# Keys and queries of a head pair loaded onto the two halves of the partitions, in a kernel of chunk-selected attention and soft mixture of experts

## The chip, the cores and the metric

The kernel runs on one core of a Trainium2 chip. The metric is the device time of one execution in microseconds (us). TensorE (PE) multiplies matrices, PEld is its loading of stationary operands, VectorE is DVE, ScalarE is ACT, GpSimd is POOL (which also issues all loads here), and SyncE (SP) issues the stores. Every engine works through its own list of instructions in order; between engines there are only semaphores.

## The reference

Attention first. For 4 batches, 8 heads, 768 rows and head size 64, the keys of a head are cut into 24 chunks of 32 rows. Each query takes an upper bound of its score against each chunk, keeps the 6 best causal chunks, and attends to the causal keys in them.

```python
k_min, k_max = k_chunks.min(axis=3), k_chunks.max(axis=3)
ub = sum(maximum(q * k_min, q * k_max), axis=-1)      # -1e9 where the chunk is in the future
top_chunks = argsort(ub)[..., -6:]
scores = scale * q @ k.T                              # -1e9 where not selected or not causal
out = softmax(scores) @ v
```

Then a soft mixture of experts over x, the 3072 x 512 result: logits = x @ phi for 32 slots, a softmax over rows makes slot inputs, 8 experts (512 to 1024 to 512, relu) work on 4 slots each, and a softmax over slots mixes their results into the 3072 x 512 output. The inputs are float32; the kernel works in bf16 on chip.

## The kernel before

The unit of work is a pair of heads, 16 pairs in all (`NPAIR`). The two heads share the 128 partitions: 64 head dimensions of each. For a pair the steps are:

- **LK, LQ, LV** (L150 to L163): POOL issues a load each for k, q and v, which casts float32 to bf16. k and q come in with partition p holding rows 6p to 6p+5 of each of the two heads, in a tile of their own (`k_in`, `q_in`, three buffers each).
- **KT and QT** (L212): twelve transposes each on PE, six row groups by two heads, into one PSUM tile (`tr_ps`, two buffers shared with other steps). **KE and QE** (L224): ACT copies that tile to `kT` or `qT` (64 dimensions of two heads by 768 rows), putting rows back into order; qT is negated.
- **KN and KX** (L234, L240): DVE reduces kT to the minimum and the maximum of each chunk. **BD** (L244) spreads these to the two heads, **QP** (L252) makes the positive part of q.
- **UB** (L260): PE makes the bounds out of qT, qp and bd. **SL, SH, UN** (L275 to L294): DVE finds the sixth largest with MAX8, POOL copies a column, DVE marks the chunks not selected. **NT, NC** (L296, L305): PE transposes the marks, DVE copies them to `nsT`.
- **S0 to S5** (L310): PE makes scores in six groups of 384 or 512 columns, with two matmuls of k and q (L317) and then two or more that add the mask out of `nsT` (L327), in a PSUM tile with two buffers. **E0 to E5** (L334): ACT takes the exponential. **A0 to A5** (L343): POOL clears the diagonal blocks.
- **P0 to P5** (L355): PE multiplies with v. **NO** (L374): DVE normalises into `x_sb`. **XT, XE**: PE transposes x, DVE copies it out; every fourth pair **LG, LC** add the logits.

The order is written out by hand. `PLAIN` and `ORDER` (L46 to L60) are lists of step names, one list for each iteration, and the code emits steps in that order, so each engine gets its own steps in it. Steps of different pairs stand in one iteration: in iteration i the scores are those of pair i, bounds and marks (UB to NC) those of pair i+1, transposes and chunk extremes (KT to BD) those of pair i+2, the k and q loads those of pair i+4, P those of pair i-1. The plain iterations 1 to 12 read

```python
PLAIN = """S0 KT S1 E0 A0 E1 LQ NO UB S2 S3 P0 KE LK SL P1 P2 P3 P4 E2 E3 A2 A1 W XT SH QT UN S4 S5 QE LV KN E4
E5 A5 A3 XE KX NT P5 NC BD QP A4 LG LC"""
```

so that ACT gets E0 E1 KE E2 E3 QE E4 E5, DVE gets NO SL UN KN XE KX NC BD QP, and PE gets S0 KT S1 UB S2 S3 P0 to P4 XT QT S4 S5 NT P5. Iterations -2, -1, 0 and 13 to 16 have lists of their own.

Expert weights (step W, L136) are loaded one matrix at a time among the iterations, 1 MB in bf16 each; 12 of the 16 have room from the start, the other four are loaded as attention buffers are given back. In w1 a partition gets two runs of two rows. After the last pair come the dispatch of the mixture (L474, which reads x with a stride of two elements as the stationary operand, to match w1), the experts (L721 to L789) and the output (L792 to L818).

## Time and profile before

| | before |
|---|---|
| times of two runs | 163.35 and 163.38 us, median 163.37 |
| span of the profiled execution, first to last instruction | 161.6 us |
| median less span | 1.77 us |
| busy: PE, DVE, ACT, POOL | 139.9, 110.3, 121.6, 95.1 us |
| mean granted TensorE clock | 0.954 |
| bytes by DMA (as landed) | 32.95 MB |

The span is what the profile shows of one execution; what is outside of it (1.77 us) is start and end of the program, and no time of that execution is listed apart from the two runs. In the rows of the timeline the first number is the start in us, the second the length in us, then engine, line, operation, out<-in with shapes, and xN for N instructions of the same kind merged; a bracket tells idle time before it and what ended it. A row without a bracket did not wait.

### The profile page before, as it was taken

What the parts mean: (1) busy time and instruction counts of PE and PEld (TensorE: products, weight loads), DVE (VectorE), ACT (ScalarE), POOL (GpSimd) and SP (SyncE); (2) the same over time, 40 slices, a digit from 0 to 9 for tenths busy, and PEclk for the clock granted to TensorE, in tenths of its full rate; (3) what the DMA queues carried; (4) which work ended last, traced back from release to release, by engine and by line L of the source; (5) the groups of instructions that cost most, each with busy time, mean ns of one, the idle gap of its engine ahead of it and who ended that gap; (6) DMA issues with size and microseconds to landing.
All of it is one profiled execution on the core that took longest, in us unless ns stands there. A gap on an engine that the chain in (4) does not pass through costs nothing.

```text
span 161.6 us, 6418 instructions
## 1 busy us (share of the span) xinstructions
PE 139.9 (87%) x2705; PEld 100.2 (62%) x2705; DVE 110.3 (68%) x379; ACT 121.6 (75%) x157; POOL 95.1 (59%) x193
## 2 busy tenths in 40 slices
PE   6559899999899999999999999999999699985500
PEld 3345566767677777666867767775689545853200
DVE  5456678879698798887888879899655432176520
ACT  3386899999899999999998999987992112085510
POOL 7968788968789687896777976685454500000000
PEclk9999999999999999999999999999999959999555
DMA  3999999999999999999999999999999998029996
GB/s 51 159 172 196 175 211 196 212 195 184 212 194 214 191 184 214 185 216 192 186 205 190 214 188 218 194 208 186 214 214 217 214 214 162 16 103 404 405 407 243
DMA packets 40477, 32.95 MB, mean 204 GB/s; under 512 B 26369, under 2 KB 34561, under 8 KB 40449
## 3 DMA queue, kind: packets, MB, share of 16 engines
q0 software_dynamic: 38432, 26.25, 109.5%
q1 hardware_dynamic: 2016, 6.29, 9.9%
q8 instruction: 21, 0.34, 0.8%
q14 instruction: 8, 0.06, 0.1%
HBM read 52.49 MB, written 6.29 MB: 364 GB/s over the span
## 4 chain that ended last, share of the span: by engine, by line
PE 54%; POOL 15%; ACT 10%; DMA 7%; issue 6%; DVE 2%; DVEq 0%; POOLq 0%; ACTq 0%
PE sc_ps L317 10%; PE at_ps L369 9%; PE sc_ps L327 7%; PE tr_ps L218 6%; POOL e_sb L345 6%; ACT e_sb L340 6%; DMA out_dram<-o_sb 5%; PE ub_ps L266 4%; PE h_ps L725 3%; DMA q_in<-in_q_dram 3%; POOL k_in L155 3%; POOL w_sb L148 2%; PE xT_ps L391 2%; POOL q_in L155 2%; PE ns_ps L299 2%
## 5 line engine op out<-in xcount | busy, mean ns | idle before, releaser
L340 ACT ACTIVATE e_sb<-sc_ps 128x768 bf16<-128x768 f32 (+1 forms) x96 | 83.2, 925 | 4.1 <-PE sc_ps L327 3.6
L345 POOL TENSOR_SCALAR_AFFINE_SELECT e_sb<-e_sb 128x256 bf16<-128x256 bf16 x96 | 36.7, 404 | 26.4 <-ACT e_sb L340 24.8
L317 PE MATMUL sc_ps<-qT,kT 64*128 64x384 bf16 (+3 forms) x288 | 39.8, 295 | 1.2 <-ACT e_sb L340 0.9
L327 PE MATMUL sc_ps<-nsT,smask 64*128 64x384 bf16 (+2 forms) x320 | 38.4, 279 | 0.2 <-issue 0.2
L369 PE MATMUL at_ps<-v_t,e_sb 128*128 128x65 bf16 x672 | 27.9, 194 | 0.3 <-issue 0.3
L369 PEld LDWEIGHTS <-e_sb 128*128 128x128 bf16 x672 | 23.9, 98 | 5.9 <-issue 5.2
L317 PEld LDWEIGHTS <-kT 64*128 64x128 bf16 x288 | 16.3, 94 | 8.5 <-issue 2.0
L327 PEld LDWEIGHTS <-smask 64*128 64x128 bf16 x320 | 17.1, 96 | 4.2 <-issue 1.2
L237 DVE TENSOR_REDUCE mm<-kT 128x24 bf16<-128x768 bf16 x16 | 15.1, 943 | 3.1 <-ACT kT L227 3.1
L160 POOL DMA_DIRECT2D v_t<-in_v_dram x16 | 16.5, 1034 | 0.0
L227 ACT ACTIVATE kT<-tr_ps 128x768 bf16<-128x768 bf16 x16 | 12.9, 806 | 4.0 <-PE tr_ps L218 4.0
L382 DVE TENSOR_TENSOR x_sb<-at_ps,inv 128x768 bf16<-128x768 f32 (+1 forms) x17 | 15.5, 910 | 0.6
L227 ACT ACTIVATE qT<-tr_ps 128x768 bf16<-128x768 bf16 x16 | 13.0, 815 | 2.8 <-PE tr_ps L218 2.6
L242 DVE TENSOR_REDUCE mm<-kT 128x24 bf16<-128x768 bf16 x16 | 15.1, 943 | 0.0
L282 DVE MAX8 mx_t<-ub_ps 128x8 f32<-128x16 f32 (+4 forms) x160 | 14.5, 164 | 0.0
L155 POOL DMA_DIRECT2D k_in<-in_k_dram x16 | 11.6, 726 | 1.4 <-POOLq L833 0.8
L155 POOL DMA_DIRECT2D q_in<-in_q_dram x16 | 11.5, 716 | 0.3 <-issue 0.2
L813 ACT ACTIVATE o_sb<-o_ps,cinv 128x512 f32<-128x512 f32 x12 | 7.9, 687 | 4.7 <-DMA out_dram<-o_sb 3.0
L278 DVE TENSOR_REDUCE mx_t<-ub_ps 128x2 f32<-128x8 f32 x16 | 2.7, 167 | 12.4 <-PE ub_ps L272 8.0
L218 PE MATMUL tr_ps<-ident,q_in 128*64 128x128 bf16 x192 | 9.1, 234 | 2.1 <-DMA q_in<-in_q_dram 1.2
L806 PE MATMUL o_ps<-so_sb,cT_all 128*128 128x256 bf16 x48 | 7.8, 288 | 3.5 <-DVE o_sb L811 2.9
L148 POOL DMA_DIRECT2D w_sb<-in_moe_w_dram x15 | 10.7, 716 | 0.1
(122 smaller groups left out, 217.0 us busy)
## 6 DMA issues: line engine op xcount, KB each, us to landing
w_sb<-in_moe_w_dram POOLq DMA_DIRECT2D x15, 1024.0 KB, 11.7
out_dram<-o_sb SPq DMA_DIRECT2D x10, 512.0 KB, 4.9
k_in<-in_k_dram POOLq DMA_DIRECT2D x16, 192.0 KB, 8.5
q_in<-in_q_dram POOLq DMA_DIRECT2D x16, 192.0 KB, 7.8
v_t<-in_v_dram POOLq DMA_DIRECT2D x16, 192.0 KB, 11.1
w_sb<-in_moe_w_dram POOLq DMA_DIRECT2D x2, 512.0 KB, 13.9
out_dram<-o_sb SPq DMA_DIRECT2D x4, 256.0 KB, 3.1
phi_sb<-in_moe_phi_dram POOLq DMA_DIRECT2D x1, 32.0 KB, 8.3
```

Source lines behind the costliest of these rows:

```text
L155: nc.gpsimd.dma_start(out=t, in_=src.rearrange("h (p g) d -> p h (g d)", p=P))
L160: nc.gpsimd.dma_start(out=v_t[i % NV][:, :, :, :D], in_=v[b, 2 * j:2 * j + 2].rearrange("h (g p) d -> p h g d", p=P),)
L218: nc.tensor.matmul(ps[h * 64:(h + 1) * 64, g, :], lhsT=src[:, h, g * D:(g + 1) * D], rhs=ident, is_transpose=True,)
L227: nc.scalar.activation(t.rearrange("d (p g) -> d p g", g=NQT), st.pop((nm + "ps", i)).rearrange("d g p -> d p g"), func=ACT.Copy, scale=-1 ...
L237: nc.vector.tensor_reduce(mm[:, 0, 0, :], kT, axis=AX.X, op=ALU.min, negate=True)
L242: nc.vector.tensor_reduce(st["mm", i][:, 1, 0, :], kT, axis=AX.X, op=ALU.max)
L317: nc.tensor.matmul(ps[:, h, c:c + w], lhsT=kT[r, kg * P:(kg + 1) * P], rhs=qT[r, qs], start=True, stop=False,)
L327: nc.tensor.matmul(ps[:, h, c + (f - t0) * P:c + (l - t0) * P], lhsT=smask[r, x, kg].rearrange("p a b -> p (a b)"), rhs=nsT[r, (f - x * NJ ...
L340: nc.scalar.activation(e[:, :, :w], st.pop(("scps", i, g))[:, :, :w], func=ACT.Exp, scale=-scale)
L345: nc.gpsimd.affine_select(out=e[:, :, :P], in_=e[:, :, :P], compare_op=ALU.is_ge, fill=0.0, base=0, pattern=[[0, 2], [1, P]], channel_mult ...
L369: nc.tensor.matmul(o, lhsT=st["e", i, g][:, h, c:c + P], rhs=v_t[i % NV][:, h, kg, :], start=(kg == 0), stop=(kg == t),)
L382: nc.vector.tensor_tensor(st["x", b][:, t0:t1, 2 * j:2 * j + 2, :].rearrange("p t h d -> p h t d"), at[:, :, :, :D], inv.broadcast_to([P, ...
```

## The change

From pair 2 on (`FIRST = 2`), k and q of a pair share one tile of twice the width: k on partitions 0 to 63, q on 64 to 127, and a partition holds twelve rows of each head rather than six. Each of the two loads of a pair then writes 64 partitions with runs twice as long. The twelve transposes called KT now take the row groups 0 to 5 of k and q together, those called QT the groups 6 to 11; the ACT copies after them write six of every twelve columns of kT and of qT, which are two halves of one tile. Pairs 0 and 1 are loaded and transposed as before, in halves of the same tiles. Both kT and qT now hold negated values, so the extremes swap their roles (max first, then the negated min), the mask's signs and the sign of the exponential's scale change, and the instruction kinds stay. The first expert matrix w1 is loaded with four rows, one run of 16 KB, for each partition; the dispatch reads x with a stride of four elements in place of two. The order lists are unchanged, and each engine gets the same number of instructions in the same order. The line numbers of the changed kernel lie 1 to 12 higher.

```diff
+    FIRST = 2
...
-            src = moe_w1[i].rearrange("(a p x) f -> p a (x f)", p=P, x=2)
-            dst = w_sb[i].rearrange("p (a f) -> p a f", a=NDG // 2)
+            src = moe_w1[i].rearrange("(p x) f -> p (x f)", x=NDG)
+            dst = w_sb[i]
...
-        t = inp.tile([P, 2, NQT * D], BF16, name=nm + "_in", tag=nm + "_in")
         src = {"k": k, "q": q}[nm][b, 2 * j:2 * j + 2]
-        nc.gpsimd.dma_start(out=t, in_=src.rearrange("h (p g) d -> p h (g d)", p=P))
-        st[nm, i] = t
+        if ("kq", i) not in st:
+            st["kq", i] = inp.tile([P, 2, 2 * NQT * D], BF16, name="kq_in", tag="kq_in")
+        if i < FIRST:
+            t = st[nm, i] = st["kq", i][:, int(nm == "q")].rearrange("p (h c) -> p h c", h=2)
+            nc.gpsimd.dma_start(out=t, in_=src.rearrange("h (p g) d -> p h (g d)", p=P))
+            return
+        half = slice(0, 64) if nm == "k" else slice(64, P)
+        nc.gpsimd.dma_start(out=st["kq", i][half], in_=src.rearrange("h (p g) d -> p h (g d)", p=64))
...
-        src = st.pop((nm, i))
+        if i < FIRST:
+            src, g0 = st.pop((nm, i)), 0
+        else:
+            src, g0 = st["kq", i], NQT * (nm == "q")
...
-                    ps[h * 64:(h + 1) * 64, g, :], lhsT=src[:, h, g * D:(g + 1) * D], rhs=ident,
+                    ps[h * 64:(h + 1) * 64, g, :], lhsT=src[:, h, (g0 + g) * D:(g0 + g + 1) * D], rhs=ident,
...
-        t = tp3.tile([P, S], BF16, name=nm + "T", tag=nm + "T")
-        nc.scalar.activation(
-            t.rearrange("d (p g) -> d p g", g=NQT),
-            st.pop((nm + "ps", i)).rearrange("d g p -> d p g"),
-            func=ACT.Copy, scale=-1.0 if nm == "q" else 1.0,
-        )
-        st[nm + "T", i] = t
+        if ("kqT", i) not in st:
+            kq = st["kqT", i] = tp3.tile([P, 2, S], BF16, name="kqT", tag="kqT")
+            st["kT", i], st["qT", i] = kq[:, 0], kq[:, 1]
+        kq, ps = st["kqT", i], st.pop((nm + "ps", i)).rearrange("d g p -> d p g")
+        if i < FIRST:
+            o = st[nm + "T", i].rearrange("d (p g) -> d p g", g=NQT)
+        else:
+            g0 = NQT * (nm == "q")
+            o = kq.rearrange("d y (p g) -> d (y p) g", g=2 * NQT)[:, :, g0:g0 + NQT]
+        nc.scalar.activation(o, ps, func=ACT.Copy, scale=-1.0)
...
-        nc.vector.tensor_reduce(mm[:, 0, 0, :], kT, axis=AX.X, op=ALU.min, negate=True)
+        nc.vector.tensor_reduce(mm[:, 0, 0, :], kT, axis=AX.X, op=ALU.max)
...
-        nc.scalar.activation(e[:, :, :w], st.pop(("scps", i, g))[:, :, :w], func=ACT.Exp, scale=-scale)
+        nc.scalar.activation(e[:, :, :w], st.pop(("scps", i, g))[:, :, :w], func=ACT.Exp, scale=scale)
...
-                xt = x.rearrange("p t h d -> p t (h d)").rearrange("p t (a c x) -> p t a x c", a=NDG // 2, x=2)
+                xt = x.rearrange("p t h d -> p t (h d)").rearrange("p t (c x) -> p t x c", x=NDG)
```

More of the change, by code (lines that the diff above doesn't have):

```diff
@@ L193 @@
             nc.gpsimd.affine_select(
-                out=squad, in_=squad, compare_op=ALU.not_equal, fill=-NEG, base=0,
+                out=squad, in_=squad, compare_op=ALU.not_equal, fill=NEG, base=0,
                 pattern=[[-CH, 2], [-64, 2], [-1, NCHUNK]], channel_multiplier=1,
@@ L197 @@
             nc.gpsimd.affine_select(
-                out=squad, in_=squad, compare_op=ALU.not_equal, fill=1.0, base=-NCHUNK,
+                out=squad, in_=squad, compare_op=ALU.not_equal, fill=-1.0, base=-NCHUNK,
                 pattern=[[-CH, 2], [-64, 2], [0, NCHUNK]], channel_multiplier=1,
@@ L241, in kmax @@
         kT = st["kT", i].rearrange("d (c x) -> d c x", x=CH)
-        nc.vector.tensor_reduce(st["mm", i][:, 1, 0, :], kT, axis=AX.X, op=ALU.max)
+        nc.vector.tensor_reduce(st["mm", i][:, 1, 0, :], kT, axis=AX.X, op=ALU.min, negate=True)
     def heads(i):
@@ L477, in dispatch @@
             for k, (x, t) in enumerate(tiles):
-                xt = x.rearrange("p t h d -> p t (h d)").rearrange("p t (a c x) -> p t a x c", a=NDG // 2, x=2)
+                xt = x.rearrange("p t h d -> p t (h d)").rearrange("p t (c x) -> p t x c", x=NDG)
                 nc.tensor.matmul(
-                    si[:, dg, :], lhsT=xt[:, t, dg // 2, dg % 2, :] if dg < NDG else ones_sq,
+                    si[:, dg, :], lhsT=xt[:, t, dg, :] if dg < NDG else ones_sq,
                     rhs=d_sb[:, k, :], start=(k == 0), stop=(k == n - 1),
```

## The prediction

> **What bounds the kernel now.** I read the page first: busy time, then the engines by slices.

> ```profile
> PE 139.9 (87%) x2705; PEld 100.2 (62%) x2705; DVE 110.3 (68%) x379; ACT 121.6 (75%) x157; POOL 95.1 (59%) x193
> ...
> ACT  3386899999899999999998999987992112085510
> ...
> PEclk9999999999999999999999999999999959999555
> ```

> Between slice 5 and slice 29 (20 to 120 us) ACT is busy eight to nine tenths or more; in the tail it hardly works. So the loop over pairs is ACT's, and the next view is ACT's timeline of one iteration, from QE (the copy of qT, L227) to the next one.

> ```profile
> 92.58 0.81 ACT L227 ACTIVATE qT<-tr_ps 128x768 bf16<-128x768 bf16 x1
> 93.29 3.21 ACT L340 ACTIVATE e_sb<-sc_ps 128x768 bf16<-128x768 f32 x4
> 96.39 0.81 ACT L227 ACTIVATE kT<-tr_ps 128x768 bf16<-128x768 bf16 x1
> 97.08 1.95 ACT L340 ACTIVATE e_sb<-sc_ps 128x1024 bf16<-128x1024 f32 x2
> 99.04 0.81 ACT L227 ACTIVATE qT<-tr_ps 128x768 bf16<-128x768 bf16 x1
> ```

> No row has a bracket: ACT never waits, and the period is its own work, 99.04 - 92.58 = 6.46 us: E4, E5, E0, E1 (93.29 to 96.39), KE, E2, E3, QE. One exponential of 1024 columns takes 0.98 of it (1.96 for two); the three of 768 take (3.10 - 0.98)/3 = 0.71 each; a copy takes 0.69 to 0.71 before the next starts.

> DVE in the same stretch:

> ```profile
> 91.19 0.94 DVE L237 TENSOR_REDUCE mm<-kT 128x24 bf16<-128x768 bf16 x1
> 92.12 0.56 DVE L402 COPY xT_sb<-xT_ps 128x768 bf16<-128x768 bf16 x1
> 92.59 0.94 DVE L242 TENSOR_REDUCE mm<-kT 128x24 bf16<-128x768 bf16 x1
> 93.80 0.36 DVE L307 COPY nsT<-ns_ps 128x384 bf16<-128x384 bf16 x1 [0.27 <-PE ns_ps L299]
> ...
> 94.24 0.36 DVE L257 TENSOR_SCALAR qp<-qT 128x768 bf16<-128x768 bf16 x1
> ```

> KN (L237) starts at 91.19, with KE long done and 1.39 us before QE even starts. That is the place to look at.

> **The change, part by part.**

> *The new wait.* Before, kT came whole out of KE. Now KE writes rows 0 to 5 of every twelve and QE the rest, so a chunk's extremes need both: KN must wait for QE to end, though the order lists are the same. In the iteration shown KN would move from 91.19 to 93.42, by 2.2 us. Behind it in DVE's queue stand XE, KX, NC, BD, QP and NO; NC's nsT is awaited by the mask matmuls of S0, these by E0 on ACT, BD and QP by UB on PE. That closes a ring: QE, KN, XE, KX, NC, S0, E0, ... QE. Its hops come from these rows:

> ```profile
> 11.14 0.81 ACT L227 ACTIVATE kT<-tr_ps 128x768 bf16<-128x768 bf16 x1 [0.45 <-PE tr_ps L218]
> ...
> 11.98 0.95 DVE L237 TENSOR_REDUCE mm<-kT 128x24 bf16<-128x768 bf16 x1 [0.15 <-ACT kT L227]
> ...
> 13.33 0.36 DVE L307 COPY nsT<-ns_ps 128x384 bf16<-128x384 bf16 x1 [0.39 <-PE ns_ps L299]
> ...
> 13.74 0.50 PE L327 MATMUL sc_ps<-nsT,smask 64*128 64x384 bf16 x2
> ```

> ```profile
> 94.30 0.34 PE L327 MATMUL sc_ps<-nsT,smask 64*128 64x384 bf16 x2
> 94.57 0.53 PE L218 MATMUL tr_ps<-ident,k_in 128*64 128x128 bf16 x12
> ...
> 95.33 0.23 PE L327 MATMUL sc_ps<-nsT,smask 64*128 64x128 bf16 x2
> ...
> 95.50 0.20 PE L266 MATMUL ub_ps<-bd,qT 128*128 128x48 bf16 x1
> ...
> 98.47 0.53 PE L218 MATMUL tr_ps<-ident,q_in 128*64 128x128 bf16 x12
> ```

> ```profile
> 104.15 0.94 DVE L237 TENSOR_REDUCE mm<-kT 128x24 bf16<-128x768 bf16 x1
> 105.01 0.94 DVE L242 TENSOR_REDUCE mm<-kT 128x24 bf16<-128x768 bf16 x1
> ...
> 106.98 0.34 DVE L307 COPY nsT<-ns_ps 128x384 bf16<-128x384 bf16 x1
> ...
> 108.28 1.51 ACT L340 ACTIVATE e_sb<-sc_ps 128x768 bf16<-128x768 f32 x2 [0.47 <-PE sc_ps L327]
> ...
> 113.95 0.36 DVE L307 COPY nsT<-ns_ps 128x384 bf16<-128x384 bf16 x1
> ```

> Count from the start of QE. KN starts 0.84 later (11.98 - 11.14, a copy and its hand-over). KN to XE 0.90 (0.93 in the row shown, with a gap), XE to KX 0.47 (92.59 - 92.12), KX to the next DVE step 0.86 (105.01 - 104.15 for the same reduction): NC starts at 3.07 and S0's mask matmuls 0.41 after it (13.74 - 13.33), at 3.48. Their results are there 0.34 later, and E0 starts at about 3.86 with the hand-over of 0.04 that QT to QE shows (98.47 + 0.53 to 99.04).

> From there two branches return to QE. On PE, S0's mask at 94.30 to QE at 99.04 is 4.74 (KT, S1, UB, S2, S3, P0 to P4, XT, QT): 3.48 + 4.74 = 8.22. On ACT, E1 waits for S1, which ends 95.33 + 0.23 - 94.30 = 1.26 after S0's mask starts, so E1 starts at 4.78; then E1 0.71, KE 0.69, E2 and E3 1.96: 8.14. UB needs QP, which starts 0.44 after NC (94.24 - 93.80) and ends 0.36 later, at 3.87; PE reaches UB at 3.48 + 1.20 = 4.68, so that is covered by 0.8 us. The period becomes 8.2 us, and ACT would idle 1.5 us of it before E0.

> QE starts at these times in iterations 0, 2 and 13:

> ```profile
> 18.97 0.81 ACT L227 ACTIVATE qT<-tr_ps 128x768 bf16<-128x768 bf16 x1
> ...
> 31.75 0.81 ACT L227 ACTIVATE qT<-tr_ps 128x768 bf16<-128x768 bf16 x1
> ...
> 105.35 0.84 ACT L227 ACTIVATE qT<-tr_ps 128x768 bf16<-128x768 bf16 x1
> ```

> Pair 2 is the first of the new kind, and its KN stands in iteration 0. From iteration 2 to 13 there are 11 periods: 11 x 8.2 = 90.2 instead of 73.6. From 1 to 2 no XE exists yet: 8.2 - 0.47 = 7.7. From 0 to 1 NC also stands ahead of KX: 7.7 - 0.86 = 6.9. These two make 14.6 instead of 12.78. Sum: (90.2 - 73.6) + (14.6 - 12.8) = 18.4 us.

> Behind iteration 13, KN (104.15, once more before QE) would start at QE + 0.84, that is 106.19 on the old scale: 2.0 us late. No DVE row from there to NC of the last pair (113.95) has a bracket, so the delay reaches that pair's scores: 2.0 us. The low end is iteration 14's E0: NC 3.68 after QE (0.84 + 104.15's own distance to 106.98, 2.83), E0 0.79 later, 4.46, instead of 108.28 - 105.35 = 2.93: 1.5 us. I take 2.0.

> *Copies with six of twelve columns written.* Reading is as before, writing is in 128 runs. The nearest rows with such writes:

> ```profile
> L340 ACT ACTIVATE e_sb<-sc_ps 128x1024 bf16<-128x1024 f32 x48 | 47.8, 1035 | 0.8 <-PE sc_ps L327 0.8
> L340 ACT ACTIVATE e_sb<-sc_ps 128x768 bf16<-128x768 f32 x48 | 38.6, 816 | 3.3 <-PE sc_ps L327 2.8
> ...
> L469 ACT ACTIVATE c_pad<-lg_all 128x288 bf16<-128x288 f32 x2 | 0.8, 444 | 0.0
> ```

> Contiguous writes cost (1035 - 816)/256 = 0.86 ns an element and 159 ns fixed, so 288 elements would take 405; written in 72 runs they took 444, 0.5 ns a run at most. 128 runs: between 0 and 70 ns a copy, twice in the ring. Taken as 0 (the same row also reads another memory); the high end is 2 x 0.07 x 13 = 1.8 us.

> *Loads.* KT needs k and q now.

> ```profile
> 5.55 0.72 POOL L155 DMA_DIRECT2D q_in<-in_q_dram  x1
> ...
> 14.81 0.85 PE L218 MATMUL tr_ps<-ident,k_in 128*64 128x128 bf16 x12
> ...
> 90.73 0.72 POOL L155 DMA_DIRECT2D k_in<-in_k_dram  x1
> ...
> DMA to landing us min/median/max: 3.4/8.5/11.0
> ...
> 55.00:80.00 25.00, 24.67 (x518) 17.96 (x513) 20.95 (x77) 24.52 (x31) 20.13 (x42) 1.00 1.48 195
> ```

> In the loop LQ is issued ahead of LK, so k stays the later one: issued at 90.73, used by the KT one period after 94.57, at 101.03, a lead of 10.3 us against a median landing of 8.5, and longer with a longer period: 0. For pair 2, q is issued at 5.55 and KT runs at 14.81: with the median it is there (14.05), with the maximum 1.7 late. Taken 0, high end 1.7. Without that cover each late load would add its lateness to one period. Half as many runs for a load are worth nothing while no engine of the loop waits for one; w1 in single runs neither, as it is used only after the last pair.

> *Stride four in the dispatch.* h_sb, read with stride four by L737, and x_sb, read with stride two:

> ```profile
> L479 PEld LDWEIGHTS <-x_sb 128*128 128x128 bf16 x96 | 3.0, 97 | 0.4 <-issue 0.3
> ...
> L737 PEld LDWEIGHTS <-h_sb 128*128 128x128 bf16 x8 | 0.5, 118 | 0.6 <-ACT h_sb L732 0.6
> ```

> At most 21 ns for each of 96 loads, 2.0 us if none overlapped; L737 lies where the clock is lower, so I take 0. Signs and extremes swap at equal instruction counts: 0.

> **Sum.** 18.4 + 2.0 = 20.4 us. The profiled span 161.6 becomes 182.0; with the 1.8 us by which the runs' median (163.4) exceeds the span: 183.8.

> **The rivals.**

> *The load stream becomes the bound (slower still).* The row 55 to 80 shows DMA engines busy all the time, 195 GB/s. A pair takes 195 GB/s x 6.7 us (73.6/11) = 1.31 MB with k and q at 0.39; if half the partitions meant half the rate, these would need 4.0 us in place of 2.0, and a pair 8.7: 11 x 0.5 = 5.5 us over the forecast, 189. Against it: weights are few in late iterations, and the rate may be set by reading, which the halves do not touch. [...]

> *The granted clock falls.* With 1.5 us idle in each period PE could lose its clock: the mask matmuls took 0.50 at 13.74 and 0.34 at 94.30, a factor 1.47. PE's 4.74 would become 7.0, the period 10.6, the time up to 183.8 + 11 x 2.4 = 210. Against it: the clock row stays 9 through the loop, and PE still works 6 us of 8.2.

> *The wait is hidden (no change).* If KN's lateness fitted into idle time of DVE and nsT still came before S0 needed it, the time stays near 163.4. Only 0.27 us of idle stands in the DVE rows before NC, against 2.2, so it decides only if KN does not in fact wait for QE.

> *The loads were the bound (faster).* If the stream set the pace and runs twice as long made k and q twice as fast, a pair would save half of their 2.0 us: 11 x 1.0 off 163.4, 152. It decides only where engines wait for loads, and ACT's rows in the loop show no wait at all.

> **How the numbers follow.** Forecast 0.79; load stream 0.07; clock 0.06; hidden 0.05; faster 0.03. The forecast's own range: period 8.05 to 8.3 (-1.7 to +1.1), end -0.5, copies +1.8, pair 2 +1.7: 181 to 188. I widen it to 178 and 191, which takes in the load stream and leaves out the clock, hidden and faster cases, 0.14 together. About 2% is what a measurement here tells from no change: faster 0.03, same 0.05, slower 0.92.

> **What would show it.** In the profile after: KN starts 0.03 us after QE ends, with a bracket that names ACT; ACT idles about 1.5 us before E0 in each iteration, waiting for the mask matmuls; QE to QE is 8.2 us in iterations 2 to 13; copies stay at 0.81 us; PE waits for no load; the tail from the last pair on keeps its length. It would be wrong if KN starts before QE ends, if QE to QE stays near 6.5, or if the copies or the PE steps grow.

## The result and the profile after

The changed kernel takes 192.1 us (median of two runs, 190.74 and 193.51) against 163.4 before: a ratio of 1.174, 95% interval 1.166 to 1.182. The forecast of 183.8 had the direction and most of the size; the range, 178 to 191, ends just below the result. The profiled execution took 190.74 us with a span of 189.0, the forecast span was 182.0, so 7.0 us are unaccounted for. Ratios here and below leave out runs more than 1.5% above the fastest of their kernel, medians do not, and five profiles (the swapped lists, the 64-column transposes, the tiny matmuls, and the early order with a late first weight, twice) are of such runs, so totals are not compared by their spans.

The page of the changed kernel: busy time, ACT and the clock by slices.

```profile
PE 148.3 (78%) x2704; PEld 105.0 (56%) x2705; DVE 111.8 (59%) x379; ACT 123.5 (65%) x157; POOL 92.3 (49%) x193
...
ACT  2558797886759696787769696767599212218530
...
PEclk9999999999699999999799997899699996999755
```

ACT, which stood at 8 and 9 through the loop, now falls to 5 to 7 in most slices, with the same work as before (123.5 us against 121.6): it waits. PE is busy 8.4 us longer with one matmul record fewer, and its clock row has dips in the loop, which the row of before had not. First the waits, on DVE's timeline of one iteration:

```profile
103.67 0.95 DVE L249 TENSOR_REDUCE mm<-kqT 128x24 bf16<-128x768 bf16 x1 [2.14 <-ACT kqT L244]
104.54 0.55 DVE L414 COPY xT_sb<-xT_ps 128x768 bf16<-128x768 bf16 x1
105.00 0.94 DVE L254 TENSOR_REDUCE mm<-kqT 128x24 bf16<-128x768 bf16 x1
105.86 0.34 DVE L319 COPY nsT<-ns_ps 128x384 bf16<-128x384 bf16 x1
```

and on ACT's, from one QE to the next:

```profile
102.82 0.82 ACT L244 ACTIVATE kqT<-tr_ps 128x768 bf16<-128x768 bf16 x1
103.53 1.72 ACT L352 ACTIVATE e_sb<-sc_ps 128x768 bf16<-128x768 f32 x2
106.72 1.71 ACT L352 ACTIVATE e_sb<-sc_ps 128x768 bf16<-128x768 f32 x2 [1.47 <-PE sc_ps L339]
108.32 0.81 ACT L244 ACTIVATE kqT<-tr_ps 128x768 bf16<-128x768 bf16 x1
109.02 1.94 ACT L352 ACTIVATE e_sb<-sc_ps 128x1024 bf16<-128x1024 f32 x2
110.98 0.82 ACT L244 ACTIVATE kqT<-tr_ps 128x768 bf16<-128x768 bf16 x1
```

QE (L244) ends at 103.64 and KN (L249) starts 0.03 us later, after 2.14 us of idle time that the bracket puts down to the copy. NC (L319) starts 3.04 us after QE, where the prediction counted 3.07, and E0 is 1.47 us late for the mask matmuls. QE to QE is 110.98 - 102.82 = 8.16 us, forecast 8.2. The ring is there, hop by hop, and the chain of work that ended last passes through these steps and back to QE by E0, E1, KE, E2 and E3.

From iteration 2 to 13 the eleven periods are 8.16, 9.68, 8.26, 8.17, 8.16, 8.17, 9.56, 8.17, 8.16, 9.65 and 8.01. Three of them are 1.4 to 1.5 us too long. The stretches view, for one ordinary period and those three (length, busy time and count of PE, PEld, DVE, ACT and POOL, then the granted clock, the DMA share and GB/s):

```profile
34.49:42.65 8.16, 6.57 (x136) 4.83 (x134) 5.75 (x20) 6.58 (x8) 4.67 (x11) 1.00 1.42 144
42.65:52.33 9.68, 8.09 (x136) 5.78 (x134) 5.69 (x20) 6.68 (x8) 6.60 (x14) 0.82 1.18 171
85.09:94.65 9.56, 8.04 (x136) 5.57 (x134) 5.72 (x20) 6.81 (x9) 5.24 (x11) 0.82 1.23 129
110.98:120.63 9.65, 8.05 (x136) 5.65 (x134) 5.70 (x20) 6.68 (x8) 5.63 (x12) 0.82 1.23 180
```

The same 136 matmuls take PE 6.57 us at clock 1.00 and 8.04 to 8.09 at 0.82, while DVE and ACT are busy about as long as in the first row. The clock changes in steps: in each of the three long periods it is 0.50 for one stretch of 3.41 us and 1.00 around it, and all its changes lie on a grid of 3.41 us. Four stretches of that grid:

```profile
44.50:47.91 3.41, 1.87 (x47) 1.40 (x46) 3.25 (x7) 1.85 (x3) 1.52 (x4) 1.00 0.85 166
47.91:51.32 3.41, 3.41 (x46) 2.35 (x45) 1.44 (x12) 2.98 (x4) 2.46 (x5) 0.50 1.50 185
...
68.39:71.80 3.41, 2.23 (x41) 1.50 (x36) 2.19 (x3) 2.79 (x4) 2.52 (x6) 1.00 0.90 133
71.80:75.22 3.42, 3.02 (x65) 2.10 (x65) 3.08 (x18) 2.47 (x4) 2.18 (x5) 1.00 1.02 204
```

The first holds PE's whole wait of 1.54 us for the mask (44.55 to 46.10): PE works 1.87 us, 0.55 of it, and the next stretch runs at half the clock. In the third the same wait (70.66 to 72.20) is cut by the border at 71.80: PE works 2.23 us, 0.65, and the clock stays. In the long period from 85.09 the idle time comes in two parts, 0.80 us that the profile gives to "issue" and 0.72 for the mask. The timeline shows where in the period, and, in its first three rows, what became of the iteration 0 to 1, which took 7.82 us in place of 6.9:

```profile
6.01 0.60 POOL L149 DMA_DIRECT2D w_sb<-in_moe_w_dram  x1
...
13.77 0.60 POOL L162 DMA_DIRECT2D kq_in<-in_q_dram  x1
...
22.54 0.53 PE L227 MATMUL tr_ps<-ident,kq_in 128*64 128x128 bf16 x12 [1.15 <-DMA kq_in<-in_q_dram]
...
49.70 1.80 PE L381 MATMUL at_ps<-v_t,e_sb 128*128 128x65 bf16 x30
...
109.02 1.12 PE L381 MATMUL at_ps<-v_t,e_sb 128*128 128x65 bf16 x30
```

The thirty P matmuls take 1.80 us in a dip and 1.12 outside of one. And KT of pair 3 at 22.54 waits 1.15 us for a load of q issued 8.8 us before, behind a whole expert matrix issued at 6.01; before, KT used k alone.

The 7.0 us: three dips 4.3 (9.68 + 9.56 + 9.65 - 3 x 8.2), iteration 0 to 1 0.9, the way from QE of iteration 13 (128.64) to the end 2.1 (60.4 instead of 56.25 + 2.0), the other periods -0.3. What stands behind each had to be tried.

### The profile page after: what moved, and what is told of

It is laid out like the page before. It is cut to its first block, busy times and chain, and to the rows that moved or that the text cites. A ratio compares the mean times of both kernels' runs of the same rounds, so it can differ in the third digit from the quotient of the medians.

```text
span 189.0 us, 6405 instructions
## 1 busy us (share of the span) xinstructions
PE 148.3 (78%) x2704; PEld 105.0 (56%) x2705; DVE 111.8 (59%) x379; ACT 123.5 (65%) x157; POOL 92.3 (49%) x193
## 3 DMA queue, kind: packets, MB, share of 16 engines
q0 software_dynamic: 33824, 26.25, 95.3%
## 4 chain that ended last, share of the span: by engine, by line
PE 30%; ACT 25%; DVE 19%; DMA 8%; issue 8%; POOL 5%; ACTq 0%; DVEq 0%; POOLq 0%
ACT e_sb L352 15%; ACT kqT L244 9%; DVE mm L249 7%; DVE mm L254 6%; PE sc_ps L339 5%; PE at_ps L381 5%; DMA kq_in<-in_q_dram 5%; PE sc_ps L329 4%; DMA out_dram<-o_sb 4%; DVE xT_sb L414 3%; PE h_ps L737 2%; PE tr_ps L227 2%; PE ub_ps L278 2%; DVE nsT L319 2%; PE at_ps L491 1%
## 5 line engine op out<-in xcount | busy, mean ns | idle before, releaser
L329 PE MATMUL sc_ps<-kqT 64*128 64x384 bf16 (+3 forms) x288 | 42.2, 311 | 1.0 <-ACT e_sb L352 0.9
L249 DVE TENSOR_REDUCE mm<-kqT 128x24 bf16<-128x768 bf16 x16 | 15.2, 953 | 34.9 <-ACT kqT L244 34.9
L244 ACT ACTIVATE kqT<-tr_ps 128x768 bf16<-128x768 bf16 x32 | 26.2, 819 | 9.5 <-PE tr_ps L227 9.3
L227 PE MATMUL tr_ps<-ident,kq_in 128*64 128x128 bf16 x384 | 18.8, 240 | 3.1 <-DMA kq_in<-in_q_dram 2.2
L329 PEld LDWEIGHTS <-kqT 64*128 64x128 bf16 x288 | 16.3, 97 | 8.5 <-issue 2.4
L227 PEld LDWEIGHTS <-kq_in 128*64 128x64 bf16 x384 | 13.2, 119 | 8.3 <-issue 5.0
L254 DVE TENSOR_REDUCE mm<-kqT 128x24 bf16<-128x768 bf16 x16 | 15.1, 943 | 0.0
L278 PE MATMUL ub_ps<-bd,kqT 128*128 128x48 bf16 x96 | 10.2, 192 | 1.2 <-DVE schunk L543 1.2
L278 PE MATMUL ub_ps<-bd,qp 128*128 128x48 bf16 x192 | 10.4, 190 | 0.4 <-ACT qp L267 0.4
L278 PEld LDWEIGHTS <-kqT 128*128 128x128 bf16 x96 | 8.3, 101 | 3.5 <-ACT kqT L244 1.4
L823 DVE TENSOR_SCALAR o_sb<-o_ps,cinv 128x512 f32<-128x512 f32 x11 | 8.0, 747 | 3.6 <-DMA out_dram<-o_sb 2.6
```

The costliest lines, as they stand in the source:

```text
L227: nc.tensor.matmul(ps[h * 64:(h + 1) * 64, g, :], lhsT=src[:, h, (g0 + g) * D:(g0 + g + 1) * D], rhs=ident, is_transpose=True,)
L244: nc.scalar.activation(o, ps, func=ACT.Copy, scale=-1.0)
L249: nc.vector.tensor_reduce(mm[:, 0, 0, :], kT, axis=AX.X, op=ALU.max)
L254: nc.vector.tensor_reduce(st["mm", i][:, 1, 0, :], kT, axis=AX.X, op=ALU.min, negate=True)
L278: nc.tensor.matmul(o, lhsT=w[:, t * P:(t + 1) * P], rhs=bd[:, x], start=(t == 0 and z == 0), stop=False,)
L329: nc.tensor.matmul(ps[:, h, c:c + w], lhsT=kT[r, kg * P:(kg + 1) * P], rhs=qT[r, qs], start=True, stop=False,)
```

## The experiments

Theory: the wait of KN for QE makes the period 8.16, and the 7.0 us are lost clock, in gaps that this wait makes, and one late load. Rivals: the half-partition loads or the interleaved copies cost something by themselves; the form of the first weights does.

**The wait without the change.** In the kernel before, KT and QT, and KE and QE, change places in the lists of iterations 0 to 13. Loads, copies and weights stay as they were; k's copy is now the later one, so KN must wait for it.

```diff
-PLAIN = """S0 KT S1 E0 A0 E1 LQ NO UB S2 S3 P0 KE LK SL ... SH QT UN S4 S5 QE LV KN E4
+PLAIN = """S0 QT S1 E0 A0 E1 LQ NO UB S2 S3 P0 QE LK SL ... SH KT UN S4 S5 KE LV KN E4
```

> The kernel before, with the names KT and QT, KE and QE exchanged in the lists of iterations 0 to 13: q is transposed and copied first, k second. Loads, layouts and copies are those of before; only KN now has to wait for the later copy. Ring theory: the same ring, a period of 8.2 us, and 184 to 190 us, the upper end if the TensorE clock also falls in some periods. Rival, the loss comes from loads or copies: 163 to 165 us.

Measured: 187.0, 195.9, 196.3 and 197.9 us, median 196.1, against 164.3 for the kernel before on that chip (no interval is given for it). Both kernels were run again beside each other on another chip:

> The kernel before, unchanged, profiled on the chip of this batch: on another chip its time spread from 163.2 to 169.3 us. All theories: ratio 1.00 within 1.5%, a period of 6.5 us, KN 1.4 us ahead of QE. If the KT of pair 3 waits for its k load here too, the wait of 1.2 us in the run with the new w1 belongs to the chip and not to w1; if not, to w1.

> The changed kernel, unchanged, on the chip of this batch, as the base for the other two: 189 to 194 us. Clock theory: the period is 8.2 us where the granted clock is 1.00 and 9.5 to 9.7 where it is near 0.82, and the number of the long ones differs from the first profile's three.

Measured: 164.5 us for the kernel before (ratio to its other runs 1.002, 0.995 to 1.009) and 194.8 us for the changed one, ratio 1.181, 1.170 to 1.192. The stretch from QE of iteration 1 to that of iteration 11, first the swapped, then the changed kernel:

```profile
28.31:116.61 88.30, 74.42 (x1390) 53.61 (x1388) 57.20 (x201) 66.15 (x81) 53.20 (x108) 0.90 1.13 152
```

```profile
28.61:116.92 88.31, 74.24 (x1390) 53.64 (x1388) 57.15 (x201) 66.22 (x81) 50.77 (x108) 0.90 1.10 151
```

Ten iterations take 88.30 and 88.31 us, at the same clock, with a first period of 7.69 and then periods of 8.15 to 8.17 and of 9.5 to 9.7 mixed in the same order. The wait alone, with the clock lost in its gaps, gives all of the loss in the loop; half-partition loads and interleaved copies add nothing to it. The swap was expected at 184 to 190. One run of four lies there, with a mean granted clock of 0.912; the three others are 6 to 8 us above, at 0.860 to 0.885, and the one of them that was profiled has six long periods of eleven, as the changed kernel beside it has, against the three of the first profile of the changed one.

**Part of the wait taken away.** The changed kernel with XE ahead of KN and KX behind NC on DVE.

```diff
-... S4 S5 QE LV KN E4 E5 A5 A3 XE KX NT P5 NC BD QP A4 LG LC"""
+... S4 S5 XE QE LV KN E4 E5 A5 A3 NT P5 NC KX BD QP A4 LG LC"""
```

> The changed kernel with two moves in the plain order list: XE goes ahead of QE's wait, KX behind NC, so that DVE gets UN XE KN NC KX BD QP. All of the change's loads, copies and waits stay. Ring theory: nsT is ready 1.7 + 0.36 us after QE starts instead of 3.1 + 0.36, E4 and E5 cover that, and the period falls from 8.2 to 6.5 or 6.6 us; with what lies outside the plain iterations (pair 3's wait for its loads 0.9, end of the loop 2 to 3, dispatch 0.8) the time is 166 to 169 us. Rival, the loads of half the partitions or the copies with gaps cost the time: it stays above 185.

Measured: 180.6 us, ratio 1.102 (1.094 to 1.109); the period is 7.43, not 6.5. DVE and one row of PE:

```profile
74.06 0.95 DVE L249 TENSOR_REDUCE mm<-kqT 128x24 bf16<-128x768 bf16 x1 [0.75 <-ACT kqT L244]
74.93 0.35 DVE L319 COPY nsT<-ns_ps 128x384 bf16<-128x384 bf16 x1
...
76.51 0.56 DVE L269 TENSOR_SCALAR qp<-kqT 128x768 bf16<-128x768 bf16 x1
...
77.12 0.22 PE L278 MATMUL ub_ps<-bd,qp 128*128 128x48 bf16 x2 [0.28 <-DVE qp L269]
```

NC (74.93) now comes right behind KN, ahead of KX, but QP has moved further back, and UB waits for it: 3.9 us from QE (73.21) to UB, 3.5 from there to the next QE. My expectation followed one branch of the ring, the one through NC, and missed the one through QP and UB, which the prediction had covered by 0.8 us.

**The clock.** The changed kernel with 24 matmuls more in S0 ahead of the mask, into columns of the PSUM tile that no step reads.

```diff
+    FILL = {i: 12 if i == 1 else 24 for i in range(1, 14) if i not in (6, 10)}
...
+            if g == 0:
+                for _ in range(FILL.get(i, 0)):
+                    nc.tensor.matmul(ps[:, 0, 384:512], lhsT=ident, rhs=ident, start=False, stop=False)
```

> The changed kernel with 24 matmuls of 128 columns (12 in iteration 1) into unused columns of S0's tile, between S0's products and its mask, in iterations 1 to 13 without 6 and 10: PE works through the 1.5 us in which it would wait for nsT. If the three periods of 9.6 us come from the granted clock, which falls after these waits, all 11 periods are 8.2 us and the time is 186 to 188 us. If they have another cause, they stay, and the time is 191 or more.

Measured: 189.1 us, ratio 1.151 (1.139 to 1.163). Ten of eleven periods are 8.01 to 8.27, and one is 9.31, with E0 2.21 us late in place of 1.47 and a stall of PE of 0.76 us that the profile gives to "issue"; from QE of iteration 2 to that of 13 it took 90.9 us, against 94.2 and 98.3 in the two profiles without fillers. But iteration 0 to 1 took 12.8 us, with KT of pair 3 waiting 4.0 for its q load at a low clock (0.74 on average from 18 to 26 us), which took part of the gain back and put the total above what the clock theory had said.

**The late load.** In the changed kernel, the first expert matrix is issued after q of pair 3 and not after q of pair 2.

```diff
-    -1: """UB KT KE SL UN QT SH NT LK QE KN PHI NC KX LQ QP BD""",
+    -1: """UB KT KE SL UN QT SH NT LK QE KN PHI NC KX LQ W0 QP BD""",
...
-    for n in "K0 Q0 K1 I Q1 K2 Q2 W G M V0 V1".split():
+    for n in "K0 Q0 K1 I Q1 K2 Q2 G M V0 V1".split():
```

> The changed kernel with the first weight matrix issued after pair 3's q load rather than after pair 2's: 2 MB less to read ahead of the loads that the KT of pair 3 waits for. If that wait (1.2 to 4 us in iteration 1) is part of the loss, it goes away and the time falls by 1 to 4 us against the changed kernel; if something else follows close behind, by less than 1.

Measured: 190.9 us, ratio 1.162 (1.152 to 1.172), 3.9 us below the changed kernel beside it. Its timeline:

```profile
13.36 0.60 POOL L162 DMA_DIRECT2D kq_in<-in_q_dram  x1
13.95 0.58 POOL L149 DMA_DIRECT2D w_sb<-in_moe_w_dram  x1
...
21.08 0.53 PE L227 MATMUL tr_ps<-ident,kq_in 128*64 128x128 bf16 x12
```

KT of pair 3 at 21.08 has no bracket, and iteration 0 to 1 takes 6.83 us; the forecast was 6.9. The swapped kernel, with whole loads and the old form of w1, also needs q first at this place, and there q's transposes wait 2.23 us for their load: the need for the later of the two loads is enough.

**Both repairs.** Fillers and late first matrix together.

> The changed kernel with both repairs that worked alone: the 24 filler matmuls in the gap ahead of S0's mask (iterations 1 to 13 without 6 and 10, 12 in iteration 1), and the first weight issued after the q load of pair 3. Theory (the forecast's mechanism was right and its sum left out the lost clock and the late load of pair 3, which are independent): iteration 0 to 1 near 7, periods of 8.15 to 8.3 in at least 10 of 11, and 184 to 187 us, near the 183.8 of the prediction. Rival (the two gains are one and the same, since the late load of pair 3 starts the row of clock losses, or the load only moves to a later pair): 188.5 or more, no better than the better of the two alone.

Measured: 184.2 us, ratio 1.129 (1.117 to 1.141). The forecast's 183.8 over 163.4 is 1.125. The stretch from QE of iteration 2 to that of iteration 11:

```profile
33.92:107.46 73.54, 70.79 (x1424) 54.59 (x1422) 51.85 (x182) 59.18 (x72) 45.34 (x97) 1.00 1.30 171
```

Nine periods in 73.54 us, 8.17 each, at clock 1.00; the two after them take 8.76, with a stall of PE of 0.50 us by "issue", and 8.01; iteration 0 to 1 takes 7.09, and from QE of iteration 13 to the end 58.2 us, where the forecast was 56.25 + 2.0. The gains add up, so they are two things, and with both gone the kernel takes what the ring says.

**The form of the first weights.** The run before, with w1 in the runs of the kernel before and the dispatch at stride two.

```diff
-            src = moe_w1[i].rearrange("(p x) f -> p (x f)", x=NDG)
-            dst = w_sb[i]
+            src = moe_w1[i].rearrange("(a p x) f -> p a (x f)", p=P, x=2)
+            dst = w_sb[i].rearrange("p (a f) -> p a f", a=NDG // 2)
```

> The run before this one with the first weights in the 2-row runs of the kernel before and the stride-two dispatch. Theory: the stride-four weight loads cost 0.15 us in each step of 18 or 24 loads, 0.8 us in all, and the runs of 16 KB cost the loads about a microsecond early on: 1 to 2 us below the run before, 182 to 185. Rival (the form of the first weights does not count): within 0.5 us of it.

Measured: 184.0 us, ratio 1.128 (1.119 to 1.138): 0.2 us less than the run before, the rival's figure. And the reverse, the kernel before with the new form of w1 and the stride of four alone:

> The kernel before with only w1 in one run of 16 KB a partition and the dispatch reading x with stride four. The loads of w1 have no waiter in the loop: 0. The dispatch: 18 matmuls took 0.60 us before and 0.75 in the changed kernel, so 5 x 0.15 to 0.2 us: 163.4 to 164.3 us. If single runs disturb the other loads, more than 165.

Measured: 167.9 us, ratio 1.022 (1.013 to 1.032), a loss that the expectation had named only as the other case. Its profile has KT of pair 3 waiting longer for k,

```profile
21.55 0.53 PE L218 MATMUL tr_ps<-ident,k_in 128*64 128x128 bf16 x12 [1.19 <-DMA k_in<-in_k_dram]
```

with an iteration 0 to 1 of 8.87 us, and a stall of PE of 1.4 us that has no releaser. The unchanged kernel before, on another chip, has 0.41 us for that wait, 6.68 for that iteration and a stall of 0.55 at that place. So the first matrix in single runs seems to hold up the loads behind it when it stands ahead of them; with the matrix issued later the form made no difference. That reading is argued from these two runs, not tried apart.

**No wait by another layout.** Loads onto half the partitions as in the change, but k and q transposed apart in 24 transposes of 64 columns each, and copied whole; w1 and dispatch as before.

```diff
+            ps = p_tp.tile([P, 2 * NQT, 64], BF16, name="tr_ps", tag="tp")
+            half = slice(0, 64) if nm == "k" else slice(64, P)
+            src = st["kq", i][half]
+            for g in range(2 * NQT):
+                for h in range(2):
+                    nc.tensor.matmul(
+                        ps[h * 64:(h + 1) * 64, g, :], lhsT=src[:, h, g * D:(g + 1) * D], rhs=ident[half, half],
+                        is_transpose=True,
+                    )
```

> The changed kernel's loads for k and q (half the partitions each, twelve rows a head), but k and q transposed apart, in 24 transposes of 64 columns each, and copied whole, so KN waits for KE alone; w1 and the dispatch as before. Ring theory: a period of 6.5 to 6.7 us again and 163 to 166 us (24 more small transposes a pair are some 0.5 us of PE, which has little room). Rival, loads on half the partitions cost the time: above 180.

Measured: 177.9 us, ratio 1.072 (1.063 to 1.082), above the ring theory's 166 and below the rival's 180. KN no longer waits for the later copy, and five of thirteen periods are 6.5 to 6.8, one is 6.9; the others are 7.6 to 9.9. Timeline of one that is long:

```profile
70.24 0.94 DVE L256 TENSOR_REDUCE mm<-kqT 128x24 bf16<-128x768 bf16 x1
...
71.85 0.81 ACT L251 ACTIVATE kqT<-tr_ps 128x768 bf16<-128x768 bf16 x1 [0.26 <-PE tr_ps L235]
...
77.21 0.22 PE L291 MATMUL ub_ps<-caus,qgrp 128*128 128x16 bf16 x3 [1.81 <-issue]
```

PE stands still for 1.81 us and nothing in the profile released it. There are ten such stalls, 0.3 to 1.8 us. Stretches from one to the next, and one of the kernel before between two of its own small ones (0.2 and 0.3 us):

```profile
52.51:58.84 6.33, 5.19 (x127) 4.08 (x128) 4.47 (x18) 4.71 (x6) 3.17 (x8) 1.00 1.31 200
58.84:64.64 5.80, 5.06 (x128) 3.81 (x128) 4.65 (x18) 4.16 (x5) 3.66 (x9) 1.00 1.32 139
64.64:77.21 12.57, 10.57 (x255) 7.88 (x256) 7.99 (x26) 11.10 (x14) 9.17 (x20) 1.00 1.18 182
```

```profile
72.89:84.83 11.94, 11.66 (x255) 8.70 (x256) 9.74 (x39) 11.32 (x15) 8.45 (x18) 1.00 1.44 194
```

Add PE's and PEld's counts: 255, 256, 511 and, before, 511. The stalls stand 256 PE instructions apart, or a multiple of it, give or take a missing record. The queue that carries instructions (packets, MB, share), here and in the kernel before:

```profile
q8 instruction: 24, 0.39, 0.9%
```

```profile
q8 instruction: 21, 0.34, 0.8%
```

That is 16 KB a packet, and PE has 3040 + 3041 instructions here, 253 a packet, in place of 2705 + 2705, 258 a packet. In the kernel before, each of its four small stalls (they end at 72.89, 84.83, 109.37 and 128.34 us) ends 1.3 to 1.5 us after one of these packets has landed (71.46, 83.50, 108.01 and 126.88). I read this as PE waiting for its next instructions; no row of the profile names that as the releaser.

**PE's instruction count without that layout.** The kernel before with 24 tiny matmuls an iteration.

```diff
+    FILL = {i: 24 for i in range(1, 14)}
...
+                    nc.tensor.matmul(ps[:, 0, 384:392], lhsT=ident, rhs=ident[:, :8], start=False, stop=False)
```

> The kernel before with 24 more tiny matmuls (8 columns each) an iteration in S0, so that PE has as many instructions a pair as in the run with the 64-column transposes, with loads, transposes and copies as before. Theory (those stalls of PE that the profile gives to no releaser are the arrival of its instruction code, 16 KB at a time, behind the loads): 24 packets of the instruction queue instead of 21, several stalls of 0.5 us or more given to issue, about 131 matmuls or a multiple apart, and 171 to 180 us. Rival (the stalls come from the 64-column transposes or the half-partition loads): only the matmuls' own time, 24 x 25 ns = 0.6 us a period, stalls of at most 0.4 us, and 168 to 171 us.

Measured: 174.2 us, ratio 1.058 (1.045 to 1.072), with 23 packets of 16 KB (24 were expected) and stalls of 0.79, 0.52, 0.33 and 0.93 us; the first three stand 256 and 2045 (eight times 256, less three) instructions apart. The stalls come without the layout, as the theory has it; they are fewer and shorter than expected. Most periods had grown to 7.23 us by the matmuls themselves; that this is why was not shown. So neither that layout nor the half-partition loads are needed for the stalls; that they are the arrival of code remains my reading, and how much of the 64-column run's loss they make is open.

**Both copies early.** In iterations 2 to 12 the transposes and copies move to the head of the iteration, with DVE's order as before. Four kernels: the changed one; with the first matrix late; with that and the old form of w1; and the kernel before with this order.

```diff
+EARLY_Q = """KT S0 KE QT S1 E0 A0 QE E1 UB LQ NO S2 S3 P0 LK SL P1 P2 P3 P4 E2 E3 A2 A1 W XT SH UN S4 S5 LV KN E4
+E5 A5 A3 XE KX NT P5 NC BD QP A4 LG LC"""
```

> The changed kernel with another order in iterations 2 to 12: both transposes of pair i+2 (KT, QT) at the head of the iteration and the two copies (KE, QE) around the first exp, so that the second copy ends before the chunk reduce's old place on DVE; the order on DVE is that of the kernel before. Theory (the wait of the chunk reduce for the second copy, and the clock lost in the gaps that it makes, are the loss; the half-partition loads and the interleaved copies cost nothing in the steady state): periods near 6.5 us, no dip of the granted clock in iterations 2 to 12, iterations 0 to 1 near 10 us as in the changed kernel, and 168 to 171 us in all. Rival A (two copies ahead of the exps delay the ring of the exps): periods of 7.2 us or more, 178 or more. Rival B (the half-partition layout has a cost of its own, as the stalls of the run with 64-column transposes could mean): periods of 6.5 with single ones of 8 to 10, 174 or more.

> The same early order, and the first weight issued after the q load of pair 3. Theory: the iteration 0 to 1 falls from near 10 us to near 6.9, so 3 to 4 us below the run with the early order alone: 164 to 167 us. Rival (the late load of pair 3 only moves a wait that comes back later, at pair 4 or 5): less than 1.5 us below it.

> The early order and the late first weight, and the first weights in the 2-row runs of the kernel before with its stride-two dispatch. Theory: the stride-four weight loads of the dispatch (0.15 us a step of 18, about 0.8 us) go, and nothing else changes: 0.5 to 1.5 us below the run before this one, 163 to 166 us, no slower than the kernel before by more than 1%. Rival (runs of 16 KB hold up other transfers all along): 2 us or more below it.

> The kernel before (its loads, transposes and copies) with the early order of QT and QE alone. Theory: its period is that of PE's and ACT's work, not of the ring through the chunk reduce, so the order changes nothing that counts: 162 to 166 us, within 1% of the kernel before. Rival (the ring through the chunk reduce bounds the kernel before too): periods below 6.3 us and 160 us or less. Rival (copies ahead of the first exp hold up the exps): 168 or more.

Measured: 178.0 us, ratio 1.087 (1.081 to 1.093); 178.3, 1.087 (1.080 to 1.093); 178.0, 1.084 (1.077 to 1.090); and for the kernel before in this order 169.3, 1.034 (1.028 to 1.039). All four figures of the theory were missed. One row of PE (S3) and DVE in the changed kernel and in the kernel before, both in the early order:

```profile
77.68 0.23 PE L331 MATMUL sc_ps<-kqT 64*128 64x128 bf16 x2 [0.66 <-ACT e_sb L354]
77.98 0.94 DVE L251 TENSOR_REDUCE mm<-kqT 128x24 bf16<-128x768 bf16 x1
79.72 0.56 DVE L416 COPY xT_sb<-xT_ps 128x768 bf16<-128x768 bf16 x1 [0.80 <-PE xT_ps L405]
```

```profile
81.36 0.23 PE L319 MATMUL sc_ps<-qT,kT 64*128 64x128 bf16 x2 [0.66 <-ACT e_sb L342]
81.66 0.94 DVE L239 TENSOR_REDUCE mm<-kT 128x24 bf16<-128x768 bf16 x1
83.39 0.56 DVE L404 COPY xT_sb<-xT_ps 128x768 bf16<-128x768 bf16 x1 [0.79 <-PE xT_ps L393]
```

KN waits for no copy, and the most frequent period is 7.12 us in both layouts: what is left over 6.5 is this order's own ring, and it is the one that the rivals named, copies that hold up the exps. S3 waits 0.66 us for E1, which now stands behind KE, E0 and QE on ACT; behind S3 stand P0 to P4, XT and S4, and E4 waits 0.75 us for S4. From 30 to 110 us the chain that ended last in the kernel before with this order holds no step of DVE, so XE's wait of 0.8 us for XT follows from this ring and does not make it. Between the two layouts the early order leaves 8.8 us of span (177.3 and 168.5), none in the ordinary periods: 3.8 in iteration 0 to 1 (10.05 and 6.22), 3.2 behind QE of iteration 13, whose list was left as it was, with KN behind QE, 2.8 in a few longer periods, and -1.0 ahead of iteration 0. Issuing the first matrix late gained nothing here: KT of pair 6 then waited 2.47 us for k, so the wait came back at a later pair, as the rival had it. No version beat the kernel before.

## Why the prediction was right, and where it was wrong

The mechanism and its place were right: KN 0.03 us after QE, NC after 3.04 us (3.07), E0 1.47 us late (1.5), period 8.16 (8.2), iteration 1 to 2 7.73 (7.7). The swap shows that the wait makes this period without anything else of the change, and 184.2 us with both repairs shows that the sum was right for what it counted, with some luck at the end of the loop, as told below.

The step that failed is the one that left the granted clock alone. The rival priced it as all or nothing, 210 us, and was given 0.06 because "the clock row stays 9 through the loop, and PE still works 6 us of 8.2". The row of a kernel without gaps says nothing on one with gaps, and the clock did not fall for good: it fell to 0.50 for one stretch of 3.41 us at a time, 1.7 us of full clock lost in a period, 1.4 to 1.5 of which the period shows, in three of eleven periods of the first profile and six of the second. In the first profile this went with how the wait for the mask lies to the grid. Of seven waits of 1.54 us two lay whole in one stretch: PE worked 0.55 of it and the next ran at 0.50, as after the two parts in the third long period. Five were cut by a border: PE worked 0.61 or more of both stretches and nothing followed. If that holds in other runs, which none tried by itself, the number of long periods, three or six, depends on where the grid happens to fall, which a sum of waits does not tell. The fillers, which take away only the idle time, bring the clock back to 1.00 and leave the period at 8.16 (42.08 to 50.24 us of the run with both repairs). The gaps ahead of the mask matmuls were at most 1.54 us.

The second step that failed is "Loads". Pair 2's KT was checked against its q load and was right (no wait); pair 3's was not. It waits 1.15 us in the first profile and 2.4 in the second, and goes with the first matrix ahead of it. The cover had been that KT used k alone; the change took it away from every pair, and the prediction looked at one of the two early ones.

The end of the loop was given 2.0; it took 2.75 to the last exponentials and 4.1 to the end. The excess of 2.1 is for the most part lost clock as well. From 130.04 to 131.86 us PE waits 1.82 us for XE, which the late KN and KX hold up in iteration 13, PE works 0.47 of that stretch of the grid, and a fourth stretch at 0.50 follows, from 133.24 to 136.66. With the late matrix alone the end takes 60.3 us, and ACT waits 0.92 us for PE there as it does in this stretch (0.91 at 136.04); with the fillers alone and with both it takes 58.0 and 58.2, without that wait. Yet the fillers do not reach PE's wait for XE, which is still 1.82 us there. So 58.2 - 56.25 = 1.95, against a forecast of 2.0, is luck in part, as I read it.

Right at nothing: the copies, 0.81 to 0.82 us as before; pair 2; and the weights' form within 0.2 us, once the first matrix was out of the way. Two readings of the prediction and one sum do not hold, though the forecast does not rest on them. In the kernel before ACT does wait in the loop, four times between iterations 2 and 13, for 0.20 to 0.66 us and each time for PE, and the chain that ended last runs through PE's steps from 94 to 105 us: that loop was PE's as much as ACT's. In the clock rival 3.48 + 7.0 is 10.5 and not 10.6, so its time would be 209.

The stride of four shows in the loads, 117 ns each where the prediction's row has 97, inside the 21 ns that it allowed:

```profile
L491 PEld LDWEIGHTS <-x_sb 128*128 128x128 bf16 x96 | 3.8, 117 | 0.4 <-issue 0.2
```

The load stream did not become the bound. The queue that carries the loads, before and after:

```profile
q0 software_dynamic: 38432, 26.25, 109.5%
```

```profile
q0 software_dynamic: 33824, 26.25, 95.3%
```

1.095 x 161.6 = 177.0 us of 16 engines before, 0.953 x 189.0 = 180.1 after, with the same bytes. Half the rate, as the rival supposed it, would have taken the k and q loads, 5.5 MB of the 26.25 (14 pairs of 0.39) and so about 37 us of the 177, to 74, an estimate of 37 us more. No run shows that half rate: the sum grew by 3, and the packets of these loads themselves took 33.7 us of 16 engines where they had taken about 36. That is no test of such a load by itself: these ran within the whole stream, which lands 195 GB/s in the prediction's row.

## What to carry to other kernels

When two producers are merged so that each writes half of what a consumer needs, the consumer waits for the later one: look for what is queued behind it, and follow every branch of the ring that this closes, not only the shortest. After a sum of waits, ask of each new idle gap on PE what it does to the clock (here by the share of 3.41 us that PE still worked, 0.55 or less against 0.60 or more in the first profile, not by the length of the gap alone), and of each load that gained a user at which pair it now comes too late. A reordering can cure such a wait and bring a ring of its own; run the kernel before in the new order as a control.
